# Stage 2 scores of an attention-into-experts kernel: key halves stacked on 128 rows, two passes instead of three

## The chip, the cores and the metric

The kernel runs on one core of a Trainium2 chip. The metric is device time in microseconds of one execution, as the median of several runs. Five engines matter: TensorE (PE, its weight loads as PEld), VectorE (DVE), ScalarE (ACT), GpSimd (POOL) and SyncE (SP), which here issues the DMAs. The program is one list of instructions for each engine, and semaphores tie the lists together.

## The reference

Eight batches of 576 tokens go through two attentions. The first is a local one with 8 heads of 64. Its output `x` (576 x 512) goes into four "experts", each a causal attention of its own with a 64-wide head, and a token's result is the mix of its two best experts.

```python
for e in range(E):                       # 4 experts
    q, k, v = x @ wq[e], x @ wk[e], x @ wv[e]
    scores = scale * (q @ k.transpose(0, 2, 1))
    scores = np.where(causal, -1000000000.0, scores)
    scores = scores - scores.max(-1, keepdims=True)
    a = np.exp(scores)
    a /= a.sum(-1, keepdims=True) + 1e-09
    ye = a @ v @ wo[e]
    # out += gate weight of e * ye, for tokens whose two best experts hold e
```

## The kernel before

Stage 1 is the windowed attention. A tile is one 64-query block of a pair of heads, four tiles are a group, and 72 groups cover the batches. `s1_qk` makes the scores (L157), their masked minimum (L162; scores are held negated), exponentials (L172) and weights (L177 on GpSimd); `s1_t` transposes (L208) and masks on the way out of PSUM (L212); `s1_av` multiplies with the values (L236). `load_pair` and `spread_q` (L68) bring the next queries.

Stage 2 works on experts in pairs, two to a 128-row tile, so there are 16 (batch, pair) combinations. Operands of the type F32R are split into a high and a low part, and a product is three passes, high x high, high x low, low x high (`three`, L298 to L300). `s2_v` projects values and gate logits, `s2_gate` picks the two best experts, `s2_k` and `s2_q` project keys and queries: ScalarE copies the high part out of PSUM, VectorE subtracts it to get the low part (L371, L372, L383, L384). A query tile holds 64 queries of the first expert against rows 0 to 63 and 64 of the second against rows 64 to 127, zeros elsewhere, so that one product gives both experts' scores of a 64-query block.

`s2_s` goes through nine such blocks. Blocks 0 to 2 are plain float32 products (L402, two instructions in a trace); blocks 3 to 8 are three passes over 64 x (block + 1) keys, the last block in two PSUM banks. VectorE adds the causal mask and takes the minimum in one instruction (L407, with a short one behind it that reads the accumulator), ScalarE makes exponentials and sums (L412). `s2_w` turns sums and gates into weights, three small VectorE instructions for a group of blocks (L424 to L426; six groups) and a GpSimd multiplication for each block (L431). `s2_t` transposes chunks of 128 keys, four to a bank (L440), which ScalarE copies out (L442). `s2_av` multiplies with the values (L461), `s2_o` with the output weights and stores.

The order is written out by hand: `half` gives each call a time within a unit by the table `POS`, and stage 1 groups are put in at 4.5 a unit; all calls are then sorted and issued. The build orders instructions within the engines' queues from there. PSUM tiles come from four rings: three buffers for the scores of both stages, two for transposes, two for projections, one for weighted values.

Of the kernel before, what the change touches and what calls it, by code (L numbers as in the profile page):

```python
# [8 lines left out]
F32 = mybir.dt.float32  # L9
F32R = mybir.dt.float32r  # L10
# [16 lines left out]
FIRST = 18              # groups of stage 1 before stage 2 has anything to do  # L27
# [6 lines left out]
def window_attention_moe_attention(ctx: ExitStack, tc: tile.TileContext, qT, kT, vW,  # L34
# [58 lines left out]
    # masks of a 64-query block and its 128 window keys, added to the negated scores; [1]: sequence start  # L93
# [20 lines left out]
    whi, wlo = {}, {}  # L114

    WEIGHTS = (("v", wv, 1040, 1.0, "pt20"), ("k", wk, 1024, 1.0, "pt21"),
               ("q", wq, 1024, -0.125, "v2"), ("o", wo, 1024, 1.0, "v2"))
    raws = {}

    def load_weights():  # L120
        for name, src, n, scale, tag in WEIGHTS:
            raw = work.tile([128, n], F32, tag=tag, bufs=2 if tag == "v2" else 1, name=f"w{name}raw")
# [8 lines left out]
    def split_weights(i):  # L131
        name, _, n, scale, _ = WEIGHTS[i]
# [19 lines left out]
    def s1_qk(g):  # L152
        while late and late[0] in pairs:
            load_v(late.pop(0))
        ps = psum.tile([128, 4, 128], F32, tag="s", bufs=3, name=f"s1_{g}")
# [32 lines left out]
    def s1_t(g):  # L188
        """Two groups share a bank (the ninth has one of its own); two tiles share a transpose."""
# [407 lines left out]
```

## Time and profile before

| | us |
|---|---|
| median of 3 runs | 547.05 (545.22 to 547.2) |
| profiled execution, first to last instruction (span) | 543.3 |
| TensorE busy | 520.7 (96%) |
| VectorE busy | 427.5 (79%) |
| ScalarE busy | 346.9 (64%) |
| GpSimd busy | 220.1 (41%) |

The span leaves out what lies before the first and behind the last instruction; it is 3.75 us under the median, and the profiled execution's own time is taken as the span and these 3.75. Busy times of TensorE count overlapping matmuls once. Durations and waits come from this one execution.

### The profile page before, as it was taken

The numbers are of one execution on the slowest core, as the hardware profiler recorded it, in microseconds if no ns is written. First come the engines' busy times: TensorE is split into PE (matmuls) and PEld (weight loads), VectorE is DVE, ScalarE is ACT, GpSimd is POOL, SyncE is SP. The second block draws the span as 40 slices with busy tenths as digits, with TensorE's granted clock in tenths as the row PEclk, the third lists the DMA queues.
The fourth block names the chain that finished last, engine by engine and source line by source line (L and its number), as shares of the span: only waits on it lengthen the run. The fifth ranks groups of instructions, "written<-read, shape, count | busy, mean of one in ns | idle before, by whom it ended". The sixth has DMA issues, their size and how long they took to land.

```text
span 543.3 us, 14011 instructions
## 1 busy us (share of the span) xinstructions
PE 520.7 (96%) x4668; PEld 462.2 (85%) x4668; DVE 427.5 (79%) x2006; ACT 346.9 (64%) x1276; POOL 220.1 (41%) x524
## 2 busy tenths in 40 slices
PE   3989999999999999999999999999999999999996
PEld 3879998988889888988889888998889988998874
DVE  4886799886979888887888979988697987754752
ACT  3887886675575856567475764666557583557561
POOL 5676454352552534444253534435255142112230
PEclk9999999999999999999999999999999999999999
DMA  8665433131522315133241424413152101100102
GB/s 297 225 187 170 123 102 112 46 94 65 149 90 85 97 61 173 48 90 92 72 142 48 130 71 136 121 47 93 64 146 73 45 2 59 40 1 21 59 1 97
DMA packets 20632, 51.23 MB, mean 94 GB/s; under 512 B 2768, under 2 KB 3280, under 8 KB 20560
## 3 DMA queue, kind: packets, MB, share of 16 engines
q1 hardware_dynamic: 20560, 50.35, 29.7%
q8 instruction: 36, 0.59, 0.5%
q14 instruction: 36, 0.29, 0.2%
HBM read 40.90 MB, written 9.44 MB: 93 GB/s over the span
## 4 chain that ended last, share of the span: by engine, by line
PE 58%; DVE 27%; ACT 8%; issue 4%; DMA 2%; POOL 1%; ACTq 0%; DVEq 0%; POOLq 0%; SPq 0%
DVE pt L212 8%; PE s L157 7%; PE o L461 7%; PE t L440 6%; DVE sm L162 3%; PE o L236 3%; ACT p L172 3%; DVE p L407 3%; PE ops L300 3%; PE ops L299 2%; PE ops L298 2%; DMA q<-in_qT_dram 2%; PE s L298 2%; PE qps L299 2%; PE qps L300 2%
## 5 line engine op out<-in xcount | busy, mean ns | idle before, releaser
L431 POOL TENSOR_SCALAR p<-p,r 128x256 f32<-128x256 f32 (+3 forms) x144 | 77.3, 547 | 143.3 <-DVE r L426 54.7
L412 ACT ACTIVATE p<-p,r 128x64 f32<-128x64 f32 (+2 forms) x144 | 80.2, 558 | 69.5 <-DVE r L407 57.1
L177 POOL TENSOR_SCALAR p<-p,st 128x64 f32<-128x64 f32 x216 | 66.5, 330 | 107.5 <-DVE st L175 68.5
L157 PE MATMUL s<-k,qbd 128*128 128x128 f32 x576 | 82.1, 287 | 10.8 <-DMA k<-in_kT_dram 4.9
L157 PEld LDWEIGHTS s<-k,qbd 128*128 128x128 f32 x576 | 74.4, 199 | 14.6 <-POOL qbd L68 5.0
L162 DVE CUSTOM_DVE_ANT_0 sm<-s,win 128x128 f32<-128x128 f32 x288 | 73.4, 281 | 15.8 <-PE s L157 14.0
L212 DVE TENSOR_TENSOR pt<-t,tri 64x512 f32<-64x512 f32 (+1 forms) x120 | 76.0, 633 | 2.6 <-PE t L208 0.2
L172 ACT ACTIVATE p<-p,st 128x64 f32<-128x64 f32 x216 | 72.2, 336 | 9.1 <-DVE p L170 5.8
L407 DVE CUSTOM_DVE_ANT_0 p<-s,causal 128x256 f32<-128x256 f32 (+7 forms) x160 | 70.9, 450 | 8.5 <-PE s L402 3.0
L442 ACT ACTIVATE pt<-t 128x512 f32<-128x512 f32 (+1 forms) x112 | 59.4, 546 | 15.4 <-PE t L440 12.8
L440 PE MATMUL t<-ident,p 128*128 128x128 f32 x400 | 64.1, 278 | 4.7 <-DVE pt L212 2.1
L461 PE MATMUL o<-pt,v 128*64 128x256 f32 (+4 forms) x512 | 58.1, 344 | 0.0
L440 PEld LDWEIGHTS t<-ident,p 128*128 128x128 f32 x400 | 45.9, 142 | 12.2 <-POOL p L431 3.4
L68 POOL TENSOR_SCALAR qbd<-q 64x576 f32<-64x576 f32 x58 | 40.4, 696 | 36.9 <-PE s L157 22.9
L461 PEld LDWEIGHTS o<-pt,v 128*64 128x64 f32 (+1 forms) x512 | 34.0, 135 | 21.5 <-issue 7.5
L236 PEld LDWEIGHTS o<-pt,v 128*64 128x64 f32 x1152 | 37.2, 137 | 9.5 <-issue 4.6
L236 PE MATMUL o<-pt,v 128*64 128x64 f32 x1152 | 43.0, 225 | 0.5 <-ACT pt L201 0.3
L298 PE MATMUL s<-kh,qh 128*128 128x256 f32 (+4 forms) x112 | 42.0, 375 | 0.0
L172 ACT ACTIVATION_READ_ACCUMULATOR p<-p,st 128x1 f32 x216 | 40.6, 188 | 0.0
L298 PE MATMUL kps<-xh,wkhi 128*128 128x320 f32 (+1 forms) x128 | 39.1, 305 | 0.0
L298 PE MATMUL qps<-xh,wqhi 128*128 128x320 f32 (+1 forms) x128 | 38.7, 302 | 0.4 <-DVE ql L384 0.4
L298 PE MATMUL v2ps<-wvhi,xh 128*128 128x260 f32 x128 | 38.2, 299 | 0.0
(120 smaller groups left out, 1345.5 us busy)
## 6 DMA issues: line engine op xcount, KB each, us to landing
v<-in_vW_dram SPq DMA_DIRECT2D x32, 576.0 KB, 4.5
k<-in_kT_dram SPq DMA_DIRECT2D x32, 320.0 KB, 3.0
q<-in_qT_dram SPq DMA_DIRECT2D x32, 288.0 KB, 3.0
out_dram<-out SPq DMA_DIRECT2D x32, 256.0 KB, 2.0
out_dram<-out SPq DMA_DIRECT2D x8, 128.0 KB, 3.1
wvraw<-in_wv_dram SPq DMA_DIRECT2D x1, 512.0 KB, 7.9
wkraw<-in_wk_dram SPq DMA_DIRECT2D x1, 512.0 KB, 7.5
wqraw<-in_wq_dram SPq DMA_DIRECT2D x1, 512.0 KB, 8.1
```

Source lines behind the costliest of these rows:

```text
L157: nc.tensor.matmul(ps[:, i], lhsT=qbd_buf[p % NQBD][:, b], rhs=pairs[p][1][:, 64 * b:64 * b + 128], start=True, stop=True)
L162: nc.vector.tensor_tensor_reduce(out=sm[:, i].rearrange("r a c -> r (a c)"), in0=ps[:, i], in1=win[:, int(b == 0)], scale=1.0, scalar=3.0e ...
L172: nc.scalar.activation(pt[:, i], pt[:, i], AF.Exp, bias=st[:, 0, i:i + 1], scale=-1.0, accum_out=st[:, 1, i:i + 1])
L177: (nc.vector if g < FIRST and i < 1 else nc.gpsimd).tensor_scalar(pt[:, i], pt[:, i], st[:, 2, i:i + 1], 1.0, op0=OP.mult, op1=OP.mult)
L212: nc.vector.tensor_mul(t[64 * w:64 * w + 64, :n, e], ps[r, :n], tri[r, w, None, :].to_broadcast([64, n, 128]))
L236: nc.tensor.matmul(o[64 * h:64 * h + 64, 4 * (k % 2) + i], lhsT=pairs[p][2][:, h, b], rhs=t[:, i, 64 * h:64 * h + 64], start=True, stop=True)
L298: nc.tensor.matmul(ps, lhsT=ah, rhs=bh, start=first, stop=False)
L407: nc.vector.tensor_tensor_reduce(out=row[:, c0:c0 + n], in0=ps[:, :n], in1=causal[:, m0:m0 + n], scale=1.0, scalar=3.0e38, op0=OP.add, op1 ...
L412: nc.scalar.activation(row, row, AF.Exp, bias=least, scale=-1.0, accum_out=r2[:, 1, i:i + 1])
L431: nc.gpsimd.tensor_scalar(row, row, r2[:, 3, x:x + 1], 1.0, op0=OP.mult, op1=OP.mult)
L440: nc.tensor.transpose(ps[:, i], P2[part][:, CH[blk, c]], ident)
L461: nc.tensor.matmul(o[64 * h:64 * h + 64, q0:n], lhsT=V2[b][:kk, c, 64 * e:64 * e + 64], rhs=PT2[part][:kk, x0:x1, h], start=c == 0, stop=c ...
```

## The change

Scores of blocks 1 to 8 are now taken for 128 queries of one expert at a time (i = 1 to 4), and the keys of an expert stand on 128 rows: the high part on its own 64 rows, the low part on the other 64 (`KS`). A first pass multiplies with queries whose other 64 rows are zero (`QZ`: high x high), a second with the stacked low and high query parts (`QS`: low x high and high x low). The copy of the high query part into the other rows is made by GpSimd. Block 0 stays a plain float32 product for both experts. The second expert's key blocks are written in reverse order; `BANKS` names what shares a PSUM bank (i, expert, column, first key, width). Rows of weights, transposes, masks, gates and values are laid out to match; odd experts' values reach swapped halves of the rows through ScalarE and GpSimd. Weights are computed for three groups instead of six. Transposed weights and values are fixed buffers, the raw weights of the start are loaded into them, and `out` has two buffers instead of three. `POS` is the same.

```diff
-WGROUPS = ((0, 3), (3, 5), (5, 6), (6, 7), (7, 8), (8, 9))
-NF = 3                  # query blocks of stage 2 whose scores are plain float32 products
...
         if j < 4:
-            nc.scalar.activation(V2[b][:, j], ps[:, :256], AF.Copy)
+            nc.scalar.activation(dst[0][:, j, :, 0], src[:, :, 0], AF.Copy)
+            vo = work.tile([128, 2, D], F32, tag="vo", bufs=2, name=f"vo_{b}_{j}")
+            nc.scalar.activation(vo, src[:, :, 1], AF.Copy)
+            for x in range(2):
+                nc.gpsimd.tensor_scalar(dst[0][64 - 64 * x:128 - 64 * x, j, :, 1], vo[64 * x:64 * x + 64],
+                                        1.0, 1.0, op0=OP.mult, op1=OP.mult)
...
     def s2_k(b, pr, half):
...
-        nc.scalar.activation(KH[b, pr][:, s], ps, AF.Copy)
-        nc.vector.tensor_sub(KL[b, pr][:, s], ps, KH[b, pr][:, s])
+        for e in range(2):
+            src = ps[64 * e:64 * e + 64].rearrange("r (a c) -> r a c", c=64)
+            dst = KS[b, pr][:, e].rearrange("r (a c) -> r a c", c=64)
+            a0, a1 = c0 // 64, (c0 + n) // 64
+            dst = dst[:, a0:a1] if e == 0 else dst[:, BLK - a1:BLK - a0][:, ::-1]
+            hi = dst[64 * e:64 * e + 64]
+            nc.scalar.activation(hi, src, AF.Copy)
+            nc.vector.tensor_sub(dst[64 - 64 * e:128 - 64 * e], src, hi)
...
     def s2_q(b, pr, half):
         ps, c0, n = proj(b, "q", pr, half)
...
+        for e in range(2):
+            r, o = slice(64 * e, 64 * e + 64), slice(64 - 64 * e, 128 - 64 * e)
+            nc.scalar.activation(QZ[pr][r, e, d], ps[r, x0:], AF.Copy)
+            nc.vector.tensor_sub(QS[pr][r, e, d], ps[r, x0:], QZ[pr][r, e, d])
+            nc.gpsimd.tensor_scalar(QS[pr][o, e, d], QZ[pr][r, e, d], 1.0, 1.0, op0=OP.mult, op1=OP.mult)
...
+    BANKS = (((1, 0, 0, 0, 256), (1, 1, 256, -64, 256)),
+             ((2, 0, 0, 0, 320), (0, 0, 320, 0, 64)),
+             ((2, 1, 0, 0, 320),),
+             ((3, 0, 0, 0, 448),),
+             ((3, 1, 0, 0, 448),),
+             ((4, 0, 0, 0, 320),),
+             ((4, 1, 0, 256, 320),),
+             ((4, 0, 0, 320, 256), (4, 1, 256, 0, 256)))
...
-                three(ps[:, :n], QH[pr][:, blk - NF], QL[pr][:, blk - NF], KH[b, pr][:, c0:c0 + n],
-                      KL[b, pr][:, c0:c0 + n], True, True)
+            nc.tensor.matmul(out, lhsT=QZ[pr][:, e, q], rhs=rhs, start=True, stop=False)
+            nc.tensor.matmul(out, lhsT=QS[pr][:, e, q], rhs=rhs, start=False, stop=True)
...
+        if k == 2:
+            s2_w(b, pr, 0)
+        if k == 4:
+            s2_w(b, pr, 1)
+        if k == 7 and not (pr == 0 and b % 2 == 0):
+            s2_w(b, pr, 2)
...
+        elif part == 0 and k == 1:
+            for e in range(2):
+                one(128 * e, 2, e, 1)
+            one(256, 1, 0, 1)
+            one(384, 2, 0, 2)
+            nc.scalar.activation(pt[:, :, 384:512], ps[:, 0:256].rearrange("r (e c) -> r e c", e=2), AF.Copy)
+            odd(256, 320)
```

In `s2_t`, a bank whose last chunks hold keys of both experts is copied out by three ScalarE instructions (one of both experts' whole chunks, two in `odd` for the 64-row remainders), block 0's by two of 64 columns, the other four banks by one each.

The order of instructions in the built programs shows where this lands. On TensorE, at the last query blocks of batch 2, first pair (`s2_2_0_8` is block 8, `kh` and `kl` the parts of the keys, `qh` and `ql` of the queries, `ops` an output product), before:

```order
L298 MATMUL s2_2_0_8_0_3146<-kh_2_0_2591,qh0_125 128x320
L299 MATMUL s2_2_0_8_0_3146<-kl_2_0_2592,qh0_125 128x320
L300 MATMUL s2_2_0_8_0_3146<-kh_2_0_2591,ql0_127 128x320
L298 MATMUL s2_2_0_8_1_3151<-kh_2_0_2591,qh0_125 128x256
L299 MATMUL s2_2_0_8_1_3151<-kl_2_0_2592,qh0_125 128x256
L300 MATMUL s2_2_0_8_1_3151<-kh_2_0_2591,ql0_127 128x256
L298 MATMUL ops_1_4_3189<-wohi_511,yh0_129 128x512
```

The same place now, with `s2_2_0_7` the last bank, which holds 256 columns of each expert:

```order
L446 MATMUL s2_2_0_7_3195<-ks_2_0_2648,qz0_128 128x256
L447 MATMUL s2_2_0_7_3195<-ks_2_0_2648,qs0_130 128x256
L446 MATMUL s2_2_0_7_3195<-ks_2_0_2648,qz0_128 128x256
L447 MATMUL s2_2_0_7_3195<-ks_2_0_2648,qs0_130 128x256
L159 MATMUL s1_38_3207<-k16_2714,qbd0_81 128x128
```

Threes over one key part each have become twos over stacked keys.

On TensorE, where the second pair's scores begin, between the transposes of the first pair (`t2`) and a value projection (`v2ps`), before:

```order
L440 MATMUL t2_2_0_0_0_3256<-ident_79,p2_0_121 128x128 x4
L402 MATMUL s2_2_1_0_0_3263<-kf_2_1_2842,qf1_134 128x64
L440 MATMUL t2_2_0_0_1_3267<-ident_79,p2_0_121 128x128 x4
L298 MATMUL v2ps_2_4_3274<-wvhi_381,xt0_2_2281 128x260
L299 MATMUL v2ps_2_4_3274<-wvlo_382,xt0_2_2281 128x260
```

And now:

```order
L498 MATMUL t2_2_0_0_0_3304<-ident_79,p2_0_122 128x128 x4
L498 MATMUL t2_2_0_0_1_3310<-ident_79,p2_0_122 128x128 x4
L446 MATMUL s2_2_1_0_3320<-ks_2_1_2899,qz1_129 128x256
L447 MATMUL s2_2_1_0_3320<-ks_2_1_2899,qs1_131 128x256
L446 MATMUL s2_2_1_0_3320<-ks_2_1_2899,qz1_129 128x256
L447 MATMUL s2_2_1_0_3320<-ks_2_1_2899,qs1_131 128x256
L319 MATMUL v2ps_2_4_3329<-wvhi_382,xt0_2_2324 128x260
```

A plain product of 64 columns has given way to the first split bank, which stands behind the transposes.

On GpSimd, around the end of the first pair's scores (`p2` score rows, `xt` and `p1` stage 1, `qbd` stage 1 queries), before:

```order
L68 TENSOR_SCALAR qbd0_81<-q18_3183 64x9x64 x2
L431 TENSOR_SCALAR p2_1_122<-p2_1_122,r2_2_0_1_3019 128x512
L252 TENSOR_SCALAR xt0_2_2281<-xh3_2482 128x4x64
L252 TENSOR_SCALAR xt1_2_2282<-xl3_2483 128x4x64
L177 TENSOR_SCALAR p1_38_3171<-p1_38_3171,st1_38_3165 128x64 x4
L177 TENSOR_SCALAR p1_39_3243<-p1_39_3243,st1_39_3237 128x64 x4
```

And now, with the query copies (`qs1`) and the odd experts' values (`v2_1`):

```order
L68 TENSOR_SCALAR qbd0_81<-q18_3230 64x9x64 x2
L254 TENSOR_SCALAR xt0_2_2324<-xh3_2535 128x4x64
L416 TENSOR_SCALAR qs1_131<-qz1_129 64x256
L254 TENSOR_SCALAR xt1_2_2325<-xl3_2536 128x4x64
L416 TENSOR_SCALAR qs1_131<-qz1_129 64x256
L179 TENSOR_SCALAR p1_38_3218<-p1_38_3218,st1_38_3212 128x64 x4
L68 TENSOR_SCALAR qbd1_82<-q19_3463 64x9x64
L179 TENSOR_SCALAR p1_39_3292<-p1_39_3292,st1_39_3286 128x64 x4
L68 TENSOR_SCALAR qbd1_82<-q19_3463 64x9x64
L340 TENSOR_SCALAR v2_1_141<-vo_3_0_3399 64x2x64 x2
```

The new copies stand between stage 1's multiplications and the copies of stage 1 queries.

## Rows read from the trace of the kernel before

**Rows 1.** The page's head: span, and each engine's busy us, share and instructions.

```profile
span 543.3 us, 14011 instructions
...
PE 520.7 (96%) x4668; PEld 462.2 (85%) x4668; DVE 427.5 (79%) x2006; ACT 346.9 (64%) x1276; POOL 220.1 (41%) x524
```

**Rows 2.** The page's chain that ended last, shares by engine.

```profile
PE 58%; DVE 27%; ACT 8%; issue 4%; DMA 2%; POOL 1%; ACTq 0%; DVEq 0%; POOLq 0%; SPq 0%
```

**Rows 3.** TensorE's waits: who waited for whom, us in total, times, longest.

```profile
PE s L157 <- DMA k<-in_kT_dram: 4.9, 1, 4.9
PE s L157 <- POOL qbd L68: 4.3, 3, 3.5
PE t L440 <- DVE pt L212: 2.1, 6, 0.4
```

**Rows 4.** TensorE's timeline: start us, duration us, line, operation, tiles, sizes, count.

```profile
521.29 0.34 PE L300 MATMUL s<-kh,ql 128*128 128x384 f32 x1
521.47 0.36 PE L298 MATMUL s<-kh,qh 128*128 128x448 f32 x1
521.67 0.36 PE L299 MATMUL s<-kl,qh 128*128 128x448 f32 x1
...
522.54 0.39 PE L300 MATMUL s<-kh,ql 128*128 128x512 f32 x1
522.77 0.31 PE L298 MATMUL s<-kh,qh 128*128 128x320 f32 x1
522.92 0.31 PE L299 MATMUL s<-kl,qh 128*128 128x320 f32 x1
...
523.21 0.29 PE L298 MATMUL s<-kh,qh 128*128 128x256 f32 x1
523.33 0.28 PE L299 MATMUL s<-kl,qh 128*128 128x256 f32 x1
```

**Rows 5.** TensorE's plain float32 products: timeline, then one form's group.

```profile
143.36 1.16 PE L157 MATMUL s<-k,qbd 128*128 128x128 f32 x8 [0.29 <-DVE r L407]
144.27 0.36 PE L299 MATMUL qps<-xl,wqhi 128*128 128x256 f32 x1
...
L402 PE MATMUL s<-kf,qf 128*128 128x192 f32 x32 | 8.7, 353 | 0.0
```

**Rows 6.** VectorE's groups by line: busy us, mean ns, then idle before.

```profile
L407 DVE CUSTOM_DVE_ANT_0 p<-s,causal 128x256 f32<-128x256 f32 (+7 forms) x160 | 70.9, 450 | 8.5 <-PE s L402 3.0 <-POOL p L177 2.6 <-PE s L300 0.9
...
L426 DVE TENSOR_TENSOR r<-r,g 128x1 f32<-128x1 f32 (+1 forms) x96 | 18.3, 190 | 1.1
L424 DVE TENSOR_SCALAR r<-r 128x1 f32<-128x1 f32 (+1 forms) x96 | 16.2, 169 | 13.2 <-ACT p L412 12.6
...
L425 DVE RECIPROCAL r<-r 128x1 f32<-128x1 f32 (+1 forms) x96 | 15.5, 161 | 0.9
L372 DVE TENSOR_TENSOR kl<-kps,kh 128x320 fp32r<-128x320 f32 (+1 forms) x32 | 14.3, 447 | 1.7 <-ACT kh L371 1.5
```

**Rows 7.** ScalarE's copies out of transposes, by form.

```profile
L442 ACT ACTIVATE pt<-t 128x512 f32<-128x512 f32 x96 | 55.6, 592 | 15.3 <-PE t L440 12.8
...
L442 ACT ACTIVATE pt<-t 128x128 f32<-128x128 f32 x16 | 4.3, 267 | 0.1
```

**Rows 8.** GpSimd: a copy's group by form, then its longest wait.

```profile
L252 POOL TENSOR_SCALAR xt<-xh 128x256 fp32r<-128x256 f32 x8 | 3.3, 412 | 7.8 <-ACT xh L244 7.7
...
POOL p L177 <- DVE st L175: 68.5, 34, 7.7
```

**Rows 9.** TensorE's timeline between a query projection and its first score.

```profile
168.66 0.31 PE L300 MATMUL qps<-xh,wqlo 128*128 128x320 f32 x1
...
181.53 0.33 PE L402 MATMUL s<-kf,qf 128*128 128x64 f32 x2
```

**Rows 10.** Busy us (instructions) of PE, PEld, DVE, ACT, POOL in one stretch, clock, DMA.

```profile
75.00:105.00 30.00, 29.18 (x290) 27.30 (x290) 27.30 (x138) 21.46 (x85) 15.24 (x37) 1.00 0.28 83
```

More of the change, by code (lines that the diff above doesn't have):

```diff
@@ L302, in s2_v @@
     def s2_v(b, j):
-        for x in (b, b + 1) if j == 4 else (b,):
-            if x not in V2:
-                V2[x] = work.tile([128, 5, E * D], F32, tag="v2", bufs=2, name=f"v2_{x}")
-        ps = psum.tile([128, 512], F32, tag="d", name=f"v2ps_{b}_{j}")
+        ps = psum.tile([128, 512], F32, tag="d", bufs=DB, name=f"v2ps_{b}_{j}")
         for c in range(NP):
@@ L417, in s2_w @@
-    def s2_w(b, pr, lo, hi):
-        part = 0 if lo < PARTS[0][1] else 1
-        i = slice(lo - PARTS[part][0], hi - PARTS[part][0])
-        r2 = R2[b, pr, part]
-        flat = P2[part].rearrange("r a c -> r (a c)")
-        gate = G2[b % 2][:, pr].rearrange("r j h -> r (j h)")[:, lo:hi]
-        nc.vector.tensor_scalar_add(r2[:, 2, i], r2[:, 1, i], 1e-9)
-        nc.vector.reciprocal(r2[:, 2, i], r2[:, 2, i])
-        nc.vector.tensor_mul(r2[:, 3, i], r2[:, 2, i], gate)
-        for blk in range(lo, hi):
-            base = 128 * CH[blk, 0]
-            row = flat[:, base:base + 64 * blk + 64]
-            x = blk - PARTS[part][0]
-            nc.gpsimd.tensor_scalar(row, row, r2[:, 3, x:x + 1], 1.0, op0=OP.mult, op1=OP.mult)
@@ L433, in s2_t @@
[L433 to L442 removed]
+        x0 = 64 if half == 0 else 0
@@ new lines, in s2_q @@
+        d = slice(c0 + x0 - 64, c0 + n - 64)
+        for e in range(2):
+            r, o = slice(64 * e, 64 * e + 64), slice(64 - 64 * e, 128 - 64 * e)
+            nc.scalar.activation(QZ[pr][r, e, d], ps[r, x0:], AF.Copy)
+            nc.vector.tensor_sub(QS[pr][r, e, d], ps[r, x0:], QZ[pr][r, e, d])
+            nc.gpsimd.tensor_scalar(QS[pr][o, e, d], QZ[pr][r, e, d], 1.0, 1.0, op0=OP.mult, op1=OP.mult)
+        if half == 0:
+            for e in range(2):
+                r = slice(64 * e, 64 * e + 64)
+                nc.scalar.activation(QF[pr][r, e], ps[r, :64], AF.Copy)
@@ new lines, in s2_w @@
+    def s2_w(b, pr, k):
+        x0, x1 = ((0, 5), (5, 7), (7, 9))[k]
+        r2 = R2[b, pr]
+        x = slice(x0, x1)
+        nc.vector.tensor_scalar_add(r2[:, 2, x], r2[:, 1, x], 1e-9)
+        nc.vector.reciprocal(r2[:, 2, x], r2[:, 2, x])
+        nc.vector.tensor_mul(r2[:, 3, x], r2[:, 2, x], G2[b % 2][:, pr, x])
+        for x in range(x0, x1):
+            i, e = (x + 1) // 2, (x + 1) % 2
+            p = PX[0][:, 0] if x == 0 else P2[i > 2][:, row(i, e):row(i, e) + 64 + 128 * i]
+            nc.gpsimd.tensor_scalar(p, p, r2[:, 3, x:x + 1], 1.0, op0=OP.mult, op1=OP.mult)
@@ new lines, in s2_t, with one, odd @@
+    def s2_t(b, pr, part, k):
+        ps = psum.tile([128, 512], F32, tag="t", bufs=TB, name=f"t2_{b}_{pr}_{part}_{k}")
+        pt = PT2[part]
+        def one(col, i, e, c):
+            at = chunk(i, e, c) if c < i else row(i, 1) - 64
+            nc.tensor.transpose(ps[:, col:col + 128], P2[part][:, at:at + 128], ident)
+        def odd(col, col0):
+            for e in range(2):
+                r = slice(64 * e, 64 * e + 64)
+                dst = pt[r, e, col0:col0 + 256].rearrange("r (a c) -> r a c", c=64)[:, 0:4:3]
+                src = ps[r, col:col + 256].rearrange("r (a c) -> r a c", c=64)[:, 1::2]
+                nc.scalar.activation(dst, src, AF.Copy)
+        if part == 0 and k == 0:
+            for e in range(2):
+                for i in (1, 2):
+                    one(256 * e + 128 * i - 128, i, e, 0)
+            nc.scalar.activation(pt[:, :, 64:320], ps.rearrange("r (e c) -> r e c", e=2), AF.Copy)
+        elif part == 0 and k == 1:
+            for e in range(2):
+                one(128 * e, 2, e, 1)
[3 more added lines that the diff above has]
+            odd(256, 320)
+        elif part == 0:
+            nc.tensor.transpose(ps[:, 0:128], PX[0].rearrange("r a c -> r (a c)"), ident)
+            for e in range(2):
+                nc.scalar.activation(pt[64 * e:64 * e + 64, e, 0:64], ps[0:64, 64 * e:64 * e + 64], AF.Copy)
+        elif k < 2:
+            for c in range(2):
+                for i in (3, 4):
+                    one(256 * c + 128 * i - 384, i, k, c)
+            nc.scalar.activation(pt[:, k, 0:512], ps, AF.Copy)
+        elif k == 2:
+            for e in range(2):
+                for i in (3, 4):
+                    one(256 * e + 128 * i - 384, i, e, 2)
+            nc.scalar.activation(pt[:, :, 512:768], ps.rearrange("r (e c) -> r e c", e=2), AF.Copy)
+        else:
+            for e in range(2):
+                one(128 * e, 4, e, 3)
+            one(256, 3, 0, 3)
+            one(384, 4, 0, 4)
+            nc.scalar.activation(pt[:, :, 832:960], ps[:, 0:256].rearrange("r (e c) -> r e c", e=2), AF.Copy)
+            odd(256, 768)
@@ L475, in s2_o @@
             three(ps, yh, yl, whi["o"][:, pr], wlo["o"][:, pr], pr == 0, pr == 1)
-        t = work.tile([128, DM], F32, tag="out", bufs=3, name=f"out_{b}_{j}")
+        t = work.tile([128, DM], F32, tag="out", bufs=2, name=f"out_{b}_{j}")
         nc.vector.tensor_copy(t, ps)
```

217 lines of the change are left out of this document (109 added, 108 removed).

## The prediction, made before the changed kernel was run

> **What bounds the kernel now.** I read the busy shares first. TensorE is busy for 520.7 of 543.3 us, VectorE for 427.5, ScalarE for 346.9, GpSimd for 220.1 [rows 1]. Matmuls overlap one another, so a busy share alone doesn't say that TensorE sets the pace. Its waits say it: the largest is one DMA wait of 4.9 us, the next 4.3 us in three pieces for the query copies of stage 1, the third 2.1 us in six [rows 3]; all of TensorE's idle time is 543.3 - 520.7 = 22.6 us, of which these two are 9.2. The chain that ended last agrees, with a reservation: 58% of it is TensorE, but 27% is VectorE [rows 2], so in about a quarter of the span VectorE is just as late. The clock is at its upper level of 2.4 GHz (granted 1.00) with TensorE at 29.18 of 30 us and VectorE at 27.30 of 30 in the same stretch [rows 10].
>
> What does TensorE's pace hang on? The starts in the timeline, not the durations, tell it. In a run of score products the next one starts 0.18 us after one of 384 columns, 0.20 after 448, 0.23 after 512, 0.15 after 320, 0.12 after 256 [rows 4], while each single one is recorded at 0.28 to 0.39 us. So the price of a product is its columns, some 0.46 ns each. The plain float32 products cost more: eight instructions of 128 columns take 144.27 - 143.36 = 0.91 us, or 0.89 ns a column, and each such product is two instructions, as the 32 instructions of the 192-column form for 16 expert pairs show [rows 5].
>
> **The change part by part.** Stage 2 works on 16 (batch, expert pair) combinations, called pairs here.
>
> *Scores, split products.* Before, six query blocks of a pair take widths 256, 320, 384, 448, 512 and 320 + 256, each in three passes: 3 x (0.12 + 0.15 + 0.18 + 0.20 + 0.23 + 0.15 + 0.12) = 3.45 us. After, the eight banks of BANKS in two passes are eight products of 256, eight of 320 and four of 448: 0.96 + 1.20 + 0.80 = 2.96 us [rows 4]. That is 0.49 us a pair, 7.8 us in 16.
>
> *Scores, plain float32.* Blocks 1 and 2 (128 and 192 columns) go over to the split form and are in the sum above; one product of 64 columns stays. Gone: 320 columns x 2 instructions x 0.89 ns = 0.57 us a pair, 9.1 us in 16 [rows 5]. TensorE's work on transposes (25 a pair) and on weighted values (the same columns) doesn't change. Sum on TensorE: -16.9 us, of it nothing beside other TensorE work.
>
> *VectorE.* Four changes. The three small instructions for the weights are done for three groups of blocks instead of six: 48 groups fewer at 169 + 161 + 190 ns, -25.0 us [rows 6]. The minima read 3,136 columns a pair instead of 2,880, at 70.9 us / (16 x 2,880) = 1.54 ns: +6.3 us. The low parts of the keys become two instructions on 64 rows for each one on 128; a row is no cheaper, so 32 more at 447 ns: +14.3 us [rows 6]. The low query parts of the first half widen by 128 columns in 32 instructions, +6.3 us at the same 1.54 ns. Sum +1.9 us, so VectorE stays at 429 us.
>
> *ScalarE.* Copies out of the transposes go from 7 to 12 a pair. Six at 592 and one at 267 ns make 3.82 us; after, four at 592, two half as wide (about 0.40 by the two rows) and six narrow ones at 267 at most: 4.77 us [rows 7]. That is +0.95 us a pair, +15 us. The keys' 32 further copies at about 0.40 us are +13, the values' 32 copies cut into two of 267 ns each +4, the exponentials over 256 more columns a pair +3.5 (at the slope between the two rows, 0.85 ns). Sum about +35 us: 382 us, some 72% of a 527 us span.
>
> *GpSimd.* 64 copies of a high query part into the other 64 rows (64x256) and 64 copies of odd experts' values (64x2x64). The nearest row is the same kind of copy of the same type, 128x256 at 412 ns [rows 8]: 128 x 0.41 = +53 us, 273 us in all, about 52%. They stand in GpSimd's queue among the multiplications by the weights and the stage 1 ones.
>
> What hides these three: TensorE's matmuls run beside them, and none of the three engines comes to its span. That cover has thin places, as in the stretch where VectorE is at 27.30 of 30 us [rows 10].
>
> *The wait that is added.* The second pass of every score product now needs ScalarE's copy and then GpSimd's. In the queue of GpSimd that copy is behind multiplications which wait for VectorE: 68.5 us in 34 waits, the longest 7.7 [rows 8]. The cover is the distance in the program: the last product of a query projection starts at 168.66 and the first score that uses it at 181.53, 12.9 us later [rows 9]; 7.7 + 0.4 fits into it. If not, everything behind that pass in TensorE's list waits with it, and VectorE's minimum of that bank too.
>
> *Waits given back.* With 16.9 us less work TensorE meets the others' results a little more often. Today's waits outside the two above are 22.6 - 9.2 = 13.4 us. The ends are none more and a doubling (13.4); I take a quarter of it, 3 us, near the lower end, since VectorE's work stays level and eight score banks a pair instead of ten pass through the three buffers. In these 3 us lies the last pair too, whose two 576-column rows come late together.
>
> **Sum.** The span of 543.3 lies 3.75 us below the median of 547.05; what lies around the span is taken as unchanged. 547.05 - 16.9 + 3 = 533 us, that is a span of about 529.4.
>
> *A rule that speaks against it.* The product of two small tiles on VectorE takes 190 ns on average, the reciprocal with one input 161 [rows 6]: 29 ns, which for GpSimd's present 220 us is next to nothing, and 24% more GpSimd work makes it 36. The Trainium skill, "SBUF — State Buffer", section "SBUF: two separate sides", says that a VectorE instruction with two SBUF inputs and a GpSimd instruction that reads SBUF shut each other out for the whole instruction. By the rows this is worth nothing in the sum; at its full price it is the second rival.
>
> **The rivals.**
> *VectorE and ScalarE share the bound.* The chain is TensorE for 58% only [rows 2]. Then 58% of 16.9 = 9.8 us come through, and ScalarE's growth counts with its part of the chain: 8% of 543 = 43 of 347 us busy, an eighth of 35 = 4.4 us. 547.05 - 9.8 + 4.4 = 542 us. For it: the 27% of VectorE. Against it: TensorE is hardly seen waiting for VectorE at all [rows 3].
> *GpSimd's copies hold VectorE up.* Each of the 128 copies stops a VectorE instruction for its 412 ns: 53 us. VectorE's part of the chain is 147 of 427 us, a third: +18 us, 547.05 - 16.9 + 18 = 548 us, no gain. This is the rule above taken at its word. Against it: the 29 ns.
> *GpSimd delivers late (the slower side).* Place: the second pass of the first score bank of a pair. It decides once the copy comes over 12.9 us after the projection [rows 9]. Price: one mean GpSimd wait, 68.5 / 34 = 2.0 us, for each of the 16 pairs is 32 us: 547.05 - 16.9 + 32 = 562 us. Against it: the longest wait on record is 7.7.
>
> **How the numbers follow.** Forecast 533 (own range 528 to 538): 0.66. Shared bound, 538 to 546: 0.17. GpSimd in VectorE's way: 0.06. GpSimd late: 0.07. The rest, 0.04, is below 528, where the fewer small VectorE instructions also shorten waits. The range of 527 to 545 holds the first, most of the second and part of the last, about 0.83 together. A measurement of this kernel can tell some 0.5% from no change, so faster is below 544.3 and slower above 549.8. Faster: 0.66 + 0.04 + 0.13 = 0.83. Same: 0.04 of the second case and 0.04 of the third, 0.08. Slower: 0.07 and the third's other 0.02, 0.09.
>
> **What would show it.** TensorE still busy over 95% with a span near 529; starts of score products 0.12, 0.15 and 0.20 us apart in pairs instead of threes; the plain product at 64 columns alone. VectorE near 429, ScalarE near 382, GpSimd near 273 us. TensorE's waits at or under 26 us, none of them large for the query copies on GpSimd. It is wrong if two-pass products start further apart than their columns say, if VectorE's busy time grows by tens of us under GpSimd, or if TensorE's waits grow by as much as its work shrinks.

## The result: 549.1 us where 533 were forecast

The changed kernel takes 549.11 us (median of 20 runs, 546.68 to 552.23) beside 546.03 us for the kernel before: a ratio of 1.0055, 95% interval 1.0038 to 1.0072. No gain at all, some 3 us of loss. The span grows by 3.4 us, from 543.3 to 546.7. The page of the profile after, busy shares and chain:

```profile
span 546.7 us, 14117 instructions
...
PE 510.7 (93%) x4588; PEld 452.3 (83%) x4588; DVE 442.1 (81%) x1922; ACT 378.4 (69%) x1428; POOL 266.5 (49%) x668
...
PE 47%; DVE 24%; ACT 16%; issue 4%; POOL 4%; DMA 3%; POOLq 0%; DVEq 0%; ACTq 0%; SPq 0%
```

Against [rows 1, 2]: TensorE is idle for 36.0 us instead of 22.6, its part of the chain went from 58 to 47%, and ScalarE's from 8 to 16%. The scores themselves run at the forecast pace. TensorE's timeline after (start, duration, line, tiles), to be held against [rows 4]:

```profile
125.66 0.28 PE L446 MATMUL s<-ks,qz 128*128 128x256 f32 x1
125.77 0.28 PE L447 MATMUL s<-ks,qs 128*128 128x256 f32 x1
125.89 0.28 PE L446 MATMUL s<-ks,qz 128*128 128x256 f32 x1
126.01 0.28 PE L447 MATMUL s<-ks,qs 128*128 128x256 f32 x1
126.13 0.31 PE L446 MATMUL s<-ks,qz 128*128 128x320 f32 x1
126.28 0.31 PE L447 MATMUL s<-ks,qs 128*128 128x320 f32 x1
```

Starts lie 0.11 to 0.15 us apart, in twos. So the saving of TensorE's columns is real, and nearly all of it was lost between products. The longest waits of TensorE's weight loads show where (who waited for whom, us in total, times, longest us):

```profile
PEld s L446 <- DVE r L460: 6.0, 10, 0.8
PEld t L498 <- POOL p L489: 5.9, 12, 1.3
PEld s L159 <- POOL qbd L68: 5.5, 3, 4.1
PEld o L554 <- ACT pt L522: 5.3, 12, 0.9
PEld s L159 <- ACT qbd L66: 4.7, 1, 4.7
PEld t L202 <- POOL sm L179: 4.4, 9, 1.4
PEld t L498 <- ACT pt L511: 2.9, 3, 1.0
PEld t L520 <- ACT pt L505: 2.9, 6, 0.7
```

The kernel before, rows of the same view:

```profile
PEld t L440 <- POOL p L431: 3.4, 6, 1.1
PEld t L200 <- POOL sm L177: 3.0, 8, 1.2
...
PEld s L157 <- DVE r L407: 2.8, 5, 0.6
PEld t L440 <- ACT pt L442: 2.3, 6, 0.6
```

The two rows of stage 1 queries (`qbd`, 5.5 and 4.7 us) belong mostly to the start and stand before as well (5.0 and 4.9). What grew comes from three engines, each for a few us in pieces under 1.5 us: the score bank that VectorE's minimum (L460) gives back, the weights from GpSimd (L489), the copies out of the transposes by ScalarE (L505, L511, L522). No row is the big one.

I measured the same thing in another way, from the starts. Between the starts of stage 1's groups 26 and 62 lie four batches; there I summed by how much each TensorE start lies later than the pace of the product ahead of it (0.109 us for a transpose or a stage 1 score of 128 columns; 0.12, 0.147, 0.175, 0.203, 0.232 us for 256 to 512 columns; weighted values and stage 2's plain products left out). Before, that is 16.7 us in 258.0; after, 27.2 in 256.2. The columns saved in four batches are half of 16.9, 8.4 us; the new lateness is 10.5. The four batches themselves became only 1.8 us shorter, so net 6.6 of the 8.4 us were lost: the weighted values, which this sum leaves out, took 3.3 us less from start to next start (49.4 and 46.1 us).

The starts of three stage 1 groups cut the run into four stretches:

| us | to group 16 | 16 to 26 | 26 to 62 | from 62 on |
|---|---|---|---|---|
| before | 46.9 | 68.0 | 258.0 | 170.4 |
| after | 49.9 | 71.7 | 256.2 | 168.9 |
| difference | +3.0 | +3.7 | -1.8 | -1.5 |
| forecast columns | 0 | -2.1 | -8.4 | -6.3 |

So the changed kernel is a little faster in most of the run and loses 6.7 us in its first 122. No stage 2 score has been issued before group 16; the last section comes back to that stretch. In the second stretch, with the first batch's scores, the granted clock is 1.00 in both kernels. TensorE's longest wait there is for GpSimd, for the second of two copies of parts of `x` that a value projection reads (L254):

```profile
92.41 0.39 PE L321 MATMUL v2ps<-wvhi,xt 128*128 128x260 f32 x1 [2.27 <-POOL xt L254]
```

GpSimd's list in front of it:

```profile
88.44 0.40 POOL L254 TENSOR_SCALAR xt<-xh 128x256 fp32r<-128x256 f32 x1
88.83 1.19 POOL L179 TENSOR_SCALAR p<-p,st 128x64 f32<-128x64 f32 x4
89.98 1.42 POOL L68 TENSOR_SCALAR qbd<-q 64x576 f32<-64x576 f32 x2
91.47 0.40 POOL L416 TENSOR_SCALAR qs<-qz 64x256 fp32r<-64x256 f32 x1
91.96 0.40 POOL L254 TENSOR_SCALAR xt<-xl 128x256 fp32r<-128x256 f32 x1
```

Between the two copies stand a stage 1 multiplication, stage 1 queries and one of the added query copies, 3.0 us in all. In the kernel before, the two copies start 1.0 us apart (81.49 and 82.44), and TensorE has no such wait.

How the smaller pieces arise can be read in the chain of waits after (start, duration, engine, tile, line, count; pieces of 0.04 us or less left out):

```profile
184.63 0.34 DVE qs L415
184.99 0.38 ACT qz L414
185.39 1.63 ACT p L469 x4
187.05 0.38 ACT pt L517
187.43 0.15 ACT pt L505
187.60 0.27 ACT pt L505
187.90 0.22 ACT kf L397
188.12 0.32 ACT ks L405
188.44 1.32 ACT p L174 x8
189.76 0.12 ACT pt L522
189.92 0.75 PE o L554 x2
```

From 184.99 to 189.88 ScalarE works without a pause: a query part, the two 576-column exponentials with their sums, narrow copies, keys, stage 1's exponentials. Behind them in its list stands the one copy (L522) for which TensorE's next weighted values wait, 0.46 us. ScalarE is busy for 69% of the span, and yet the chain runs through it here for 4.9 us.

### The profile page after: what moved, and what is told of

It is laid out like the page before. It is cut to its first block, busy times and chain, and to the rows that moved or that the text cites. A ratio compares the mean times of both kernels' runs of the same rounds, so it can differ in the third digit from the quotient of the medians.

```text
span 546.7 us, 14117 instructions
## 1 busy us (share of the span) xinstructions
PE 510.7 (93%) x4588; PEld 452.3 (83%) x4588; DVE 442.1 (81%) x1922; ACT 378.4 (69%) x1428; POOL 266.5 (49%) x668
## 4 chain that ended last, share of the span: by engine, by line
PE 47%; DVE 24%; ACT 16%; issue 4%; POOL 4%; DMA 3%; POOLq 0%; DVEq 0%; ACTq 0%; SPq 0%
PE o L554 6%; DVE pt L214 6%; PE s L159 6%; ACT p L174 5%; PE t L498 5%; PE o L238 4%; DVE p L460 3%; ACT p L464 3%; PE s L446 3%; DVE sm L164 3%; PE v2ps L319 3%; DMA q<-in_qT_dram 2%; DVE ks L406 2%; PE v2ps L321 2%; ACT p L469 2%
## 5 line engine op out<-in xcount | busy, mean ns | idle before, releaser
L489 POOL TENSOR_SCALAR p<-p,r 128x192 f32<-128x192 f32 (+3 forms) x128 | 73.2, 587 | 62.9 <-DVE r L485 38.3
L460 DVE CUSTOM_DVE_ANT_0 p<-s,causal 128x320 f32<-128x320 f32 (+3 forms) x160 | 73.3, 472 | 12.5 <-PE s L447 10.9
L464 ACT ACTIVATE p<-p,r 128x192 f32<-128x192 f32 (+2 forms) x96 | 53.4, 557 | 41.1 <-DVE r L460 40.7
L416 POOL TENSOR_SCALAR qs<-qz 64x256 fp32r<-64x256 f32 x64 | 26.4, 413 | 78.4 <-ACT qz L414 55.0
L498 PE MATMUL t<-ident,p 128*128 128x128 f32 x384 | 58.3, 279 | 5.2 <-ACT pt L511 2.3
L446 PE MATMUL s<-ks,qz 128*128 128x256 f32 (+2 forms) x160 | 55.1, 355 | 2.8 <-DVE r L460 2.8
L554 PE MATMUL o<-pt,v 128*64 128x256 f32 (+3 forms) x512 | 54.3, 340 | 2.3 <-ACT pt L522 2.3
L498 PEld LDWEIGHTS t<-ident,p 128*128 128x128 f32 x384 | 42.8, 140 | 14.8 <-POOL p L489 5.9
L554 PEld LDWEIGHTS o<-pt,v 128*64 128x64 f32 x512 | 38.2, 136 | 19.2 <-ACT pt L522 5.3
L447 PE MATMUL s<-ks,qs 128*128 128x256 f32 (+2 forms) x160 | 48.3, 312 | 0.0
L238 PEld LDWEIGHTS o<-pt,v 128*64 128x64 f32 x1152 | 38.1, 140 | 8.7 <-DVE yl L561 1.4
L414 ACT ACTIVATE qz<-qps 64x256 fp32r<-64x256 f32 x64 | 24.1, 377 | 23.9 <-PE qps L321 15.3
```

The lines of the kernel that those rows point to most:

```text
L238: nc.tensor.matmul(o[64 * h:64 * h + 64, 4 * (k % 2) + i], lhsT=pairs[p][2][:, h, b], rhs=t[:, i, 64 * h:64 * h + 64], start=True, stop=True)
L446: nc.tensor.matmul(out, lhsT=QZ[pr][:, e, q], rhs=rhs, start=True, stop=False)
L460: nc.vector.tensor_tensor_reduce(out=dst, in0=ps[:, col:col + n], in1=mask, scale=1.0, scalar=3.0e38, op0=OP.add, op1=OP.min, accum_out=least)
L464: nc.scalar.activation(whole, whole, AF.Exp, bias=least, scale=-1.0, accum_out=r2[:, 1, x:x + 1])
L489: nc.gpsimd.tensor_scalar(p, p, r2[:, 3, x:x + 1], 1.0, op0=OP.mult, op1=OP.mult)
L498: nc.tensor.transpose(ps[:, col:col + 128], P2[part][:, at:at + 128], ident)
```

## The experiments

Times are medians beside the kernel before on the same chip (545.7 to 546.2 us). "Kept order" means that each engine's instructions were chained in the order of the kernel named, because the scheduler orders a changed program anew. Parts 2 and 4 and the query copies of part 3 have only runs in the scheduler's new order; a difference of a few us in them can be the order's.

**1. Are TensorE's columns what counts?** Third pass left out in the kernel before, second pass left out in the changed one:

```diff
-  three(ps[:, :n], QH.., QL.., KH.., KL.., True, True)
+  matmul(ps[:, :n], lhsT=QH.., rhs=KH.., start=True, stop=False)
+  matmul(ps[:, :n], lhsT=QH.., rhs=KL.., start=False, stop=True)
-  matmul(out, lhsT=QZ.., rhs=rhs, start=True, stop=False)
-  matmul(out, lhsT=QS.., rhs=rhs, start=False, stop=True)
+  matmul(out, lhsT=QZ.., rhs=rhs, start=True, stop=True)
```

> The kernel before with the third pass (low query part times high key part) of every split score product left out; every copy, minimum and wait stays. That takes 16 x 3.45 / 3 = 18.4 us of columns from TensorE. If the kernel before is bound by TensorE, nearly all of it comes through: 528 to 532 us. If VectorE and ScalarE share the bound (58% of the chain is TensorE): -10.7, about 535. If TensorE's columns do not count at all: 546.

> The kernel before with the third pass of every split score product left out and every engine's instructions kept in the order of the kernel before. 18.4 us of columns go from TensorE; with the scheduler's new order 7.9 us of it came through. If the order ate the rest: 529 to 533 us. If the bound is shared: 537 to 541.

> The changed kernel with the second pass of every split score product left out; the copies stay, the wait for the GpSimd copy is gone. That takes 16 x 1.48 = 23.7 us of columns from TensorE. If the changed kernel is still bound by TensorE (the two-pass products cost more than their columns): 525 to 530 us. If the other engines' chains set its pace, most of it is turned into waits: 540 to 548.

> The changed kernel with the second pass of every split score product left out, as in the run with one pass, but with every engine's instructions kept in the changed kernel's own order (the scheduler had put them in another order there). 23.7 us of columns go from TensorE. If the scheduler's new order ate the saving: 528 to 538 us. If the other engines' chains hold TensorE back in any order: 545 to 549.

Measured: before, 538.17 us (ratio 0.9854, 0.9832 to 0.9875) in the new order and 540.82 (0.9891, 0.9867 to 0.9915) in the kept one; changed, 547.38 (1.0032, 1.0015 to 1.0050) and 551.17 (1.0095, 1.0071 to 1.0119). So in the kernel before 18.4 us of TensorE's work are worth 5 to 8 us; in the changed one 23.7 us are worth nothing. The order did not eat it: with the order kept, less came through, not more, and 551.2 lies above the 545 to 549 expected. A lower granted clock can have taken a small part (last section). The page of the changed kernel with one pass in the kept order:

```profile
span 548.3 us, 13796 instructions
...
PE 494.6 (90%) x4428; PEld 432.9 (79%) x4428; DVE 443.2 (81%) x1922; ACT 378.9 (69%) x1428; POOL 266.7 (49%) x668
...
PE 36%; DVE 30%; ACT 19%; issue 6%; POOL 4%; DMA 3%; POOLq 0%; ACTq 0%; DVEq 0%; SPq 0%
```

TensorE's part of the chain falls from 47 to 36%, and VectorE and ScalarE take it over: the time doesn't fall. The lateness of starts in the four batches rises from 27.2 to 39.2 us, by as much as the columns that went there (half of 23.7).

**2. Is it the zeroing at the start?** QZ, PT2 and V2 zeroed by VectorE.

```diff
-  nc.gpsimd.tensor_scalar(t[r, e], ident[r, 0:1]...  # QZ; PT2, V2: nc.gpsimd.memset
+  nc.vector.tensor_scalar(t[r, e], ident[r, 0:1]...  # QZ; PT2, V2: nc.vector.memset
```

> The changed kernel with the zeroing of the query tiles (QZ), the transposed weights (PT2) and the values (V2) on VectorE instead of GpSimd. If these stand in the way of stage 1's first multiplications and cost the 3 us by which the kernel is late at 46 us: 546 us, and the TensorE clock stays at 1.00 in the first 25 us. If the start is late for another reason (the clock, a DMA): 549.

547.65 us (1.0033, 1.0016 to 1.0050): its interval overlaps that of the changed kernel, so this is unclear, and the clock did not stay at 1.00 (0.86 in the first 25 us). In its profile group 16 starts at 48.6 us instead of 49.9, with the same 0.86 in both, so the zeroing may be worth some 1.3 of the 3.0 us. See the last section.

**3. Work moved between engines.** The second high query copy by ScalarE; the odd copies out of the transposes by VectorE; the odd experts' values by ScalarE alone.

```diff
-  nc.gpsimd.tensor_scalar(QS[pr][o, e, d], QZ[pr][r, e, d], 1.0, 1.0, ...)
+  nc.scalar.activation(QS[pr][o, e, d], ps[r, x0:], AF.Copy)
-  nc.scalar.activation(dst, src, AF.Copy)            # odd()
+  nc.vector.tensor_copy(dst, src)
-  nc.scalar.activation(vo, src[:, :, 1], AF.Copy)    # and two GpSimd copies of vo
+  nc.scalar.activation(dst[0][64-64*x:128-64*x, j, :, 1], src[64*x:64*x+64, :, 1], AF.Copy)
```

> The changed kernel with the second copy of the high query part written by ScalarE from the bank instead of by GpSimd: GpSimd 64 copies less (-26 us, 240), ScalarE 64 more (+26, 404). If the queue of GpSimd gives the gain back (first batch, xt behind qs): 543 to 546 us. If ScalarE's extra copies give it back: 551 to 555. If neither: 549.

> The changed kernel with the four odd copies of a pair out of the transposes on VectorE instead of ScalarE: ScalarE 64 copies of 64x128 less (about -15 us), VectorE 64 more (about +12, 454). If ScalarE alone gives the gain back: 541 to 543. If VectorE counts as much as ScalarE: 548 to 551.

> The changed kernel with the four odd copies of a pair on VectorE instead of ScalarE, each at the place in the order at which the scheduler of the changed kernel had put it, all else in the changed kernel's order. With the scheduler's new order it took 566.9 us. If that was the order: 546 to 553. If it was the 12 us of work on VectorE: 560 to 567.

> The changed kernel with the odd experts' values copied straight from the bank by two ScalarE instructions, instead of one ScalarE and two GpSimd ones: GpSimd 64 copies less (-26 us), ScalarE 32 narrow ones more (about +7, 385). If the queue of GpSimd is what holds the first batch and the weights up: 545 to 547. If ScalarE's work decides (0.6 us for each us): 552 to 554.

> The changed kernel with the odd experts' values copied straight from the bank by two ScalarE instructions and none on GpSimd, in the changed kernel's order. With the scheduler's new order it took 558.9 us. If that was the order: 545 to 550 (GpSimd has 26 us less, ScalarE 7 more). If it was ScalarE's work: 556 to 560.

Measured: query copies 564.39 us (1.0342); odd copies 566.89 (1.0371), in the kept order 556.45 (1.0183, 1.0157 to 1.0208); values 558.91 (1.0227), kept 557.38 (1.0189, 1.0163 to 1.0214). In the new order all three came out above every range expected. Two things follow. Of the 18 us that the odd copies on VectorE cost, 10 are the scheduler's new order and 7 the work: ScalarE -14.3, VectorE +16.2 us busy. And moving the values costs 8 us for 13.7 us more on ScalarE, although GpSimd has 20 us less: GpSimd's queue alone, one of the explanations that I expected, is not what holds this kernel. How much of the 15 us of the query copies (27.6 us more on ScalarE) is their new order, no run shows.

**4. One part of the change in the kernel before.** Copies out of the transposes in halves; weights in three groups.

```diff
-  nc.scalar.activation(dst, ps[:, :len(sub)], AF.Copy)
+  for x in range(2):
+      nc.scalar.activation(dst[:, :, 64*x:64*x+64], ps[:, :len(sub), 64*x:64*x+64], AF.Copy)
-WGROUPS = ((0, 3), (3, 5), (5, 6), (6, 7), (7, 8), (8, 9))
+WGROUPS = ((0, 5), (5, 8), (8, 9))
```

> The kernel before with every copy out of the transposes of stage 2 cut into two half as wide: 112 ScalarE instructions more, about +15 us of ScalarE (112 x about 0.4 us less 112 x half of 0.59), nothing else. If ScalarE's work counts as it did in the run with the query copies on ScalarE (15 us for 26): +8 to +9 us, 554 to 555. If ScalarE has cover before the change (64% busy): 546 to 548.

> The kernel before with the weights of stage 2 done in three groups of blocks (0-4, 5-7, 8) instead of six, which is this one part of the change: 48 groups of three small VectorE instructions fewer, -25 us of VectorE, and some weights later. If VectorE shares the bound with TensorE: 538 to 543. If VectorE's work is hidden: 546. If the later weights cost more: over 548.

Copies 544.74 us (0.9972, 0.9956 to 0.9987), weights 547.90 (1.0035, 1.0017 to 1.0052). The first added only 5.0 us to ScalarE's busy time (346.9 to 351.9), so it tests less than I meant; it costs nothing and lies below both ranges expected. The second took only 12.0 us from VectorE (427.5 to 415.5) where I had 25, and gave nothing back. Two of its rows, one each of the addition and the product, for five columns at a time, beside [rows 6]:

```profile
L424 DVE TENSOR_SCALAR r<-r 128x5 f32<-128x5 f32 x16 | 2.6, 164 | 3.2 <-ACT p L412 3.0
L426 DVE TENSOR_TENSOR r<-r,g 128x5 f32<-128x5 f32 x16 | 2.6, 161 | 0.3
```

Half the groups are gone, and the rest are recorded at 0.15 to 0.23 us each, about as before: the durations of the three lines fall from 49.8 to 26.5 us, by 23.3, but VectorE's busy time only by 12.0. Taking out the additions alone (parts 5 and 6 below) took 75 and 52% of their durations from the busy time. So the records of short instructions overlap their neighbours' (in the kernel before all of VectorE's durations add up to 535 us, and it is busy for 427.5), and their mean durations must not be added up.

**5. Three of the engines relieved in the changed kernel, in its own order.** Low query parts left out (VectorE); the long exponentials left out, the weights of these rows then come from the minima (ScalarE); the additions of 1e-9 left out (VectorE).

```diff
-  nc.vector.tensor_sub(QS[pr][r, e, d], ps[r, x0:], QZ[pr][r, e, d])
-  nc.scalar.activation(whole, whole, AF.Exp, bias=r2[:, 0, 7 + e:8 + e], ...)   # 576 columns, twice
-  nc.vector.tensor_scalar_add(st[:, 2], st[:, 1], 1e-9)                         # and r2 alike
```

> The changed kernel, in its own order, with VectorE's low query parts left out (their rows are zeroed once at the start): 64 VectorE instructions of 0.42 us, -27 us, fewer; TensorE and ScalarE keep all their work. If VectorE's queue sets the changed kernel's pace: 525 to 536 us. If TensorE or ScalarE alone does: 546 to 549.

> The run without low query parts with the second pass of the split score products left out as well (-27 us of VectorE, -23.7 us of TensorE columns), in the changed kernel's order. If VectorE goes on setting the pace: the same as the run without low query parts alone. If TensorE becomes the bound once VectorE has room: 10 to 20 us below it.

> The changed kernel, in its own order, with the two 576-wide exponentials of each pair left out (the weights of these rows then come from the minima): 32 ScalarE instructions of 0.77 + 0.19 us, -31 us, fewer. If ScalarE's queue sets the pace as much as VectorE's: 529 to 539 us. If VectorE alone does: 546 to 549.

> The changed kernel, in its own order, without the additions of 1e-9 to the sums of the exponentials in stages 1 and 2 (each sum is at least 1, where the float32 addition changes nothing): 120 small VectorE instructions of 0.15 to 0.23 us fewer, at most -29 us. If VectorE's queue sets the pace: 533 to 541 us. If it does not: 547 to 549.

> The changed kernel, in its own order, with three things left out together that gave 0 to 4 us each alone: the second pass of the split scores (TensorE -23.7 us), the low query parts (VectorE -27; their rows are zeroed once, by VectorE) and the two 576-wide exponentials (ScalarE -31). If the end is set in turn by all engines, so that each one alone is covered by the next: 520 to 535 us, at least twice the sum of the three single gains. If one thing that none of the three touches (the transfers, GpSimd's queue, a fixed latency) holds the period of two batches near 127 us: 541 to 547.

Measured: low parts 549.06 us (1.0056), with one pass 547.97 (1.0024), exponentials 545.49 (0.9981, 0.9964 to 0.9998), additions 547.02 (1.0017, 0.9997 to 1.0038); passes, low parts and exponentials together 536.90 (0.9847, 0.9822 to 0.9871). The first two carry a start that is 3.5 us later in their profiles (stage 1's group 8 at 33.3 instead of 29.8 us), since GpSimd zeroes four more tiles ahead of stage 1's first multiplications; taking the whole 3.5 us for that, I estimate 545.6 and 544.5 without it. In the run of all three VectorE does that zeroing, and the start is as in the changed kernel (group 26 at 121.2 instead of 121.6 us). So against 549.1 the single ones give -2.1 (one pass, part 1), 3.5 and 3.6 us, 5.0 in sum, and the three together 12.2; their 536.9 us lie just outside the 520 to 535 expected. In the period of the four batches alone (256.2 us after) it is 257.2 with one pass, 254.1 without low parts, 254.5 without long exponentials, 251.6 without all three: 2.8 us in sum and 4.6 together. Both are more than the sum, one by over twice, the other by 1.6 times: the engines cover one another, though by how much is less sure. What no run took out alone is GpSimd's work, so its part is open.

**6. What the runs point to.** The kernel before, with the halved copies (part 4) and without the additions in stage 1 and stage 2, in the order of the halves:

```diff
-  nc.vector.tensor_scalar_add(st[:, 2], st[:, 1], 1e-9)                         # stage 1
-  nc.vector.reciprocal(st[:, 2], st[:, 2])
+  nc.vector.reciprocal(st[:, 2], st[:, 1])
-  nc.vector.tensor_scalar_add(r2[:, 2, i], r2[:, 1, i], 1e-9)
-  nc.vector.reciprocal(r2[:, 2, i], r2[:, 2, i])
+  nc.vector.reciprocal(r2[:, 2, i], r2[:, 1, i])
```

> The kernel before with the copies out of the transposes in halves (544.7 us alone) and without the additions of 1e-9 to sums that are at least 1 (168 small VectorE instructions fewer), in the order that the scheduler gave the halves. If VectorE is on the path for a quarter of the span: 540 to 543 us. If the next engine covers it: 544 to 546.

539.82 us (0.9887, 0.9870 to 0.9904): it beats both kernels, and its page shows a version that is nearer to TensorE's bound:

```profile
span 537.7 us, 13968 instructions
...
PE 519.6 (97%) x4668; PEld 461.6 (86%) x4668; DVE 409.2 (76%) x1838; ACT 351.6 (65%) x1388; POOL 222.3 (41%) x524
...
PE 82%; DVE 8%; POOL 3%; DMA 3%; ACT 2%; issue 2%; POOLq 0%; SPq 0%; DVEq 0%; ACTq 0%
```

TensorE carries 82% of the chain here, against 58% in [rows 2], with VectorE at 409 instead of 427.5 us. The lateness of starts in the four batches is 14.2 us. Against the halves alone, in the same order, 16.2 us less on VectorE gave 4.9 us, 30%, although VectorE had only 18% of the chain there. On this version the same saving on TensorE should be worth more; that wasn't run.

## Why the prediction was wrong, point by point

The changed kernel saved the 16.9 us of TensorE's columns that were forecast. The step that failed is the term for the waits: 3 us were put down for what TensorE waits more, and by the profiles it was 20.3 (16.9 saved, and yet 3.4 us more span), above the 13.4 taken for the upper end: 3.0 us up to group 16, 5.8 with the first batch's scores, 6.6 in the four batches, 4.8 behind them. What is not shown is how these divide among the added work, the order and the clock. The scheduler's order alone moved the time by up to 10 us in the experiments, `POS` was left as it was, and no other order of the changed kernel was run.

- **"TensorE bounds"**, from idle 22.6 us [rows 1, 3]: the step that carried the rest, and too strong. Busy time counts a product's recorded 0.28 to 0.39 us, so lateness between starts that are 0.12 us apart hides in it. The Trainium skill, "Perfetto Trace Analysis", section "Identifying the Most-Contended Engine", says that TensorE's matmul busy share is no good measure of how near a kernel is to its peak, and names two others, one of them the busy share of the weight loads. The first half agrees with the runs. The share of the weight loads doesn't help here: that share is 85% in the kernel before, where TensorE has 58% of the chain, and 86% in the best version, where it has 82%. The 58% in [rows 2] said it better, and still too much: 5.3 to 7.5 of 18.4 us came through (29 to 41%) even where nothing was added.
- **"Waits given back: 3 us"**, the term that failed. In four of the eight batches alone the lateness of starts grew by 10.5 us, or 6.6 net, where 8.4 us of columns went. The reason given for the low value, level work on VectorE and fewer score banks, looked at one engine; ScalarE's +31.5 us and GpSimd's +46.4 stand in lists ahead of copies that TensorE waits for, as the two places above show.
- **Scores, -16.9 us on TensorE**: right in pace.
- **VectorE +1.9 us**: it is +14.6 (442.1). The term at fault is the -25.0 us of small instructions, which measured -12.0 in the run with that part alone. With this the step gives +14.9. The minima, key and query parts came to +5.9, +14.8 and +4.2 where +6.3, +14.3 and +6.3 were forecast. The minima after, first from the page, then with the key and query parts by form:

```profile
L460 DVE CUSTOM_DVE_ANT_0 p<-s,causal 128x320 f32<-128x320 f32 (+3 forms) x160 | 73.3, 472 | 12.5 <-PE s L447 10.9
```

```profile
L415 DVE TENSOR_TENSOR qs<-qps,qz 64x256 fp32r<-64x256 f32 x64 | 26.8, 420 | 5.2 <-ACT qz L414 4.1
...
L406 DVE TENSOR_TENSOR ks<-kps,ks 64x320 fp32r<-64x320 f32 x32 | 15.6, 488 | 4.7 <-ACT ks L405 4.0
L406 DVE TENSOR_TENSOR ks<-kps,ks 64x256 fp32r<-64x256 f32 x32 | 13.5, 422 | 2.4 <-ACT ks L405 0.9
...
L460 DVE CUSTOM_DVE_ANT_0 px<-s,m_f 128x64 f32<-128x64 f32 x16 | 3.5, 218 | 1.9 <-PE t L520 1.9
```

  The minima and the key parts before are in [rows 6] (70.9 and 14.3); the query parts before:

```profile
L384 DVE TENSOR_TENSOR ql<-qps,qh 64x128 fp32r<-64x128 f32 (+1 forms) x64 | 22.6, 353 | 12.6 <-ACT qh L383 10.6 <-PE s L300 1.0
```

- **ScalarE +35, GpSimd +53**: +31.5 and +46.4. The sizes were right; "what hides these three" was not. The groups of ScalarE's narrow copies and of GpSimd's query copy:

```profile
L505 ACT ACTIVATE pt<-t 64x128 f32<-64x128 f32 x64 | 17.1, 268 | 0.7
...
L522 ACT ACTIVATE pt<-t 64x64 f32<-64x64 f32 x32 | 6.8, 213 | 0.5
...
L416 POOL TENSOR_SCALAR qs<-qz 64x256 fp32r<-64x256 f32 x64 | 26.4, 413 | 78.4 <-ACT qz L414 55.0 <-DVE st L177 20.4 <-PE t L520 1.1
```

- **The added wait**: covered as forecast. The query copies are in no row of TensorE's waits. But they make GpSimd stand for ScalarE, 55.0 us in all, ahead of other work; the wait of 2.27 us for the copy of `x` came from such a queue. I priced what waits for the copy, not what is queued behind it.
- **The rivals.** "VectorE and ScalarE share the bound" had the mechanism, with 542 us too little: it scaled TensorE's saving by the chain (58%, where 29 to 41% came through, which would be 5 to 7 of the 16.9 us) and ScalarE's growth by an eighth, 4.4 us. By difference everything else that came with the change costs 8 to 10 us; that is not measured alone, but 13.7 us more on ScalarE cost 8 in experiment 3, not 2. "GpSimd's copies hold VectorE up" came near in time (548) by luck: its price was 53 us of VectorE, and VectorE's excess of 12.7 us over the forecast is about the weights' 13.0. Taking 20 us of GpSimd away left VectorE at 440.4. The rule of the Trainium skill, "SBUF — State Buffer", section "SBUF: two separate sides", thus shows no visible price here. The product of two small tiles, from which the prediction argued, takes 188 ns instead of 190. "GpSimd delivers late" did occur, not at the query copies but at the weights (5.9 us), in stage 1 (4.4) and at the copy of `x` in the first batch.
- **The checks named**: "waits grow by as much as its work shrinks" is the one that came true; TensorE's share fell to 93%, under the 95% named.
- **The base**: three runs gave 547.05 us before, twenty give 546.03, so the base was 1.0 us high. And the 3.75 us that were taken to lie around the span mix two executions: the runs on record have 1.7 to 3.7 us there. The forecast time doesn't depend on it, the forecast span does.

## What to carry to other kernels

In a kernel like this one, with TensorE, VectorE and ScalarE busy for 96, 79 and 64% and GpSimd for 41%, a share of busy time is not what a saving is worth. The share of the chain came nearer for TensorE (58%; 29 to 41% came through), but it is no fixed rate either: for VectorE 18% stood in the chain and 30% came through. Work added to a "free" engine is paid where it stands ahead of something that the bound engine waits for. Measure the slack of a pipelined engine by its starts against its pace, not by its idle time. Before a large saving on one engine is written, try it cheaply by leaving the work out: here that run would have said 5 to 8 us, before anything was paid for it. And look at the first batch by itself: here it lost more than any other.

## What the runs showed of the hardware that was not expected

The profiled start differs from run to run with the clock. First 25 us (busy of PE, PEld, DVE, ACT, POOL; granted clock; DMA), kernel before:

```profile
0.00:25.00 25.00, 15.95 (x136) 14.34 (x136) 15.81 (x70) 15.39 (x52) 14.50 (x50) 1.00 0.75 260
```

The changed kernel:

```profile
0.00:25.00 25.00, 14.77 (x99) 13.38 (x100) 14.05 (x70) 13.16 (x43) 15.27 (x62) 0.86 0.73 256
```

The kernel before with two passes in the kept order (0.93 in the next 25 us too, where the other two have 1.00):

```profile
0.00:25.00 25.00, 14.91 (x106) 13.08 (x106) 15.04 (x67) 14.15 (x47) 15.75 (x50) 0.93 0.74 256
```

The clock has two levels here, 2.4 and 1.2 GHz; 0.86 over 25 us is the lower one for some 7 us (2 x 0.14 x 25). Stage 1's group 16 starts at 46.9, 49.9 and 49.9 us in the three, and the third issues the same instructions as the first up to its first scores. So it isn't shown that the 3 us that the changed kernel's profile loses before any score come from the change. In all three TensorE had been waiting for transfers and query copies just before; what decides between the two levels there is not settled.

Each run's mean granted clock is on record too. Of the changed kernel's 20 runs the three at 0.998 took 546.7 to 546.9 us and the two at 0.981 552.2; the median is 0.992. Of 94 runs of the kernel before that were made beside the experiments, 32 are at 0.998 or more and took 544.5 to 547.1 us, median 545.6. So at like clocks the change costs some 1.3 us instead of 3, by few runs, and the rest goes with a lower clock; whether the change brings that about is open. The runs with one pass have a median of 0.987: that is 5.5 us more at the lower level than at 0.992 (2 x 0.005 x 547), which costs at most half of that, as work takes up to twice as long there: 2.7 of the 23.7 us.

Keeping or renewing the scheduler's order of the same instructions moved the time by 2.6, 3.8 and 10.4 us in three pairs of runs, in both directions; in the fourth the 1.5 us are within the intervals.
